# Fused gated linear attention and gated convolution network: the first k/q load behind a clearing, its multiplication in two, a fifth weight tile split without TensorE, and new instruction sequences

## The chip, the cores and the metric

The kernel runs on one core of one Trainium2 chip. The metric is the device time of one execution in microseconds (us); of several runs the median is taken. The core has five engines with instruction queues of their own: TensorE (PE in the profile, its weight loads PEld), VectorE (DVE), ScalarE (ACT), GpSimd (POOL) and SyncE (SP). An instruction starts when the ones before it on its engine have been issued and the semaphores that it waits for have come. DMA transfers are issued here by SP, and two of them by ScalarE; they run beside the engines.

## The reference

Inputs are q, k, v and f_logit of shape 4 x 8 x 768 x 48 (batch, heads, sequence, head size), and the weights moe_w_in (384 x 1024), moe_conv_w (3 x 1024) and moe_w_out (1024 x 384). The weights arrive as float64. Cut to what is computed:

```
f = 1 / (1 + exp(-f_logit))
for t in range(S):
    state = f[t] * state + outer(k[t], v[t])        # per batch and head, 48 x 48
    x[t]  = q[t] @ state                            # the heads side by side: 384 features
h    = relu(x @ w_in)                               # 768 x 1024 per batch
c[s] = conv_w[0]*h[s-1] + conv_w[1]*h[s] + conv_w[2]*h[s+1]
out  = (h * sigmoid(c)) @ w_out                     # 768 x 384 per batch
```

## The kernel before, in words

**Attention.** The sequence of each of the 4 batches is cut into 6 chunks of 128 positions: 24 steps n, each over all 8 heads (4 pairs p of heads). A step takes the logarithm of the gate (ScalarE, L532 Exp and L536 Ln), sums it along the chunk, forms e and its inverse (ScalarE, L567 with + and L569 with -, the two halves of tile e), and multiplies the k half and the q half of tile kq by them (VectorE, L573). For the steps of the first three groups (9 steps) the sum along the chunk is a TensorE product with a triangle of ones (L558, into a PSUM tile mm); for the others VectorE scans (L565). TensorE then turns k (L588, into PSUM tile Y; copied to kp by L599), forms the scores (L595, into S; masked into am by VectorE, L603), the rank products of k and v (L623), the products with the masked scores (L615) and with the carried state (L659). The state itself goes through L634, L636, L639 and L645. The result is kept as a high part (ScalarE, L672) and a low part (VectorE, L674) in xT, and six small DMAs (L682) gather the rest of the rows after every third step.

**Network.** For each half of a batch (384 positions) and each of 8 blocks of 128 inner features, nine products with high and low parts (L712) give h; ScalarE applies relu (L722) and the middle tap (L728), VectorE the two other taps (L732, twice), ScalarE the tanh of the gate (L736), VectorE the gate's product (L738). For each of 24 tiles of 128 positions ScalarE and VectorE form the high and low part (L755, L759), and 24 products (L768: 16 with the high part gh, 8 with the low part gl) give the output tile, which is copied (L774) and stored (L778). The first L768 of all needs all of w_out split.

**Splitting the weights.** A float64 weight is split into a high and a low part by integer operations (`split_f64`, L393 to L461). There are three tiles of w_in (two blocks of 512 columns each, 1024 elements a row) and four of w_out (768 elements a row). The character of `ez` for a tile sets its way. 'd': VectorE L418, L421, L431, L446; ScalarE L437 (high part); then for each of two halves TensorE joins three terms (L454 in fp32, L455 and L456 in fp32r) and ScalarE copies the sum out of PSUM (L459). 'r': VectorE L416, L418, L421, L424, L427, L429 and ScalarE L426; TensorE has no part in it. Before, the three tiles of w_in go by 'd' and the four of w_out by 'r'.

**What sets the order.** A planner (`class Plan`) holds every piece of work with its needs and buffers. `ORDER` (L35 on) lists them one after another; in `fixed` and `trace` they are issued in just this order, each into the queue of its engine, and a number behind a point says which buffer of a ring is taken. So `ORDER` fixes the sequence on every engine and of SP's DMAs. SP has at most 8 transfers under way: each DMA issue from the ninth on waits for the one eight before it.

**The start.** VectorE clears tile stir (L307), and TensorE multiplies it with itself (L383): two products of 512 and 320 columns and 12 more of 256 (`MORE`, L388), which compute nothing that is used; the planner places the 12 like other work. ScalarE's first instruction is the load of kq for step 0 (L379, 512 KB), its second the load of its function table (L380). SP begins with the gates of the first steps (L517, fb, 192 KB each).

## Time and profile before

| | |
|---|---|
| runs | 304.17, 305.18, 309.48 us; median 305.18 |
| profiled execution | 303.35 us, span 301.5 us (1.85 us lie around the span) |
| TensorE | busy 293.0 us, 97% of the span |
| VectorE | busy 254.1 us, 84% |
| ScalarE | busy 244.7 us, 81% |
| DMA | 43.38 MB, mean 144 GB/s over the span |
| granted TensorE clock | 1.00 (2.4 GHz) in all slices |

The profile shows one execution. Its page gives busy times, the span in slices, the chain of work that ended last, the costliest groups of instructions by line, and the DMA issues. Further views are asked of the same trace: the waits of an engine (who ended its idle time), the timeline (instructions in order of time), and the busy time of each engine in stretches. The sum of idle and busy time of the engine that is busy nearly always says what can be won from it; of another engine one reads when it has its results ready.

### The profile page before, as it was taken

The numbers are of one execution on the slowest core, as the hardware profiler recorded it, in microseconds if no ns is written. First come the engines' busy times: TensorE is split into PE (matmuls) and PEld (weight loads), VectorE is DVE, ScalarE is ACT, GpSimd is POOL, SyncE is SP. The second block draws the span as 40 slices with busy tenths as digits, with TensorE's granted clock in tenths as the row PEclk, the third lists the DMA queues.
The fourth block names the chain that finished last, engine by engine and source line by source line (L and its number), as shares of the span: only waits on it lengthen the run. The fifth ranks groups of instructions, "written<-read, shape, count | busy, mean of one in ns | idle before, by whom it ended". The sixth has DMA issues, their size and how long they took to land.

```text
span 301.5 us, 10045 instructions
## 1 busy us (share of the span) xinstructions
PE 293.0 (97%) x4319; PEld 275.4 (91%) x4319; DVE 254.1 (84%) x408; ACT 244.7 (81%) x493; POOL 2.8 (1%) x16
## 2 busy tenths in 40 slices
PE   6989999999999999999999999999999999999994
PEld 3877788999999999999999999999999999999993
DVE  3789999999999998998999997978796497599361
ACT  4778889999887999999899688796995877866740
POOL 3000000000000000000000000000000000000000
PEclk9999999999999999999999999999999999999999
DMA  7968699731420335742661236318340240323311
GB/s 257 390 248 260 206 309 400 216 110 44 120 86 1 99 109 163 222 157 72 231 174 68 72 73 208 107 47 267 113 143 11 73 150 0 116 103 123 96 54 58
DMA packets 19269, 43.38 MB, mean 144 GB/s; under 512 B 2685, under 2 KB 10005, under 8 KB 19221
## 3 DMA queue, kind: packets, MB, share of 16 engines
q1 hardware_dynamic: 18932, 41.98, 42.8%
q8 instruction: 35, 0.57, 0.8%
q10 hardware_dynamic: 288, 0.72, 0.7%
q14 instruction: 14, 0.11, 0.1%
HBM read 35.61 MB, written 4.72 MB: 134 GB/s over the span
## 4 chain that ended last, share of the span: by engine, by line
PE 88%; ACT 4%; DMA 3%; DVE 2%; SPq 1%; issue 1%; ACTq 0%
PE mm L712 33%; PE mm L768 32%; PE Y L615 4%; PE S L595 4%; PE Y L659 4%; PE Y L623 3%; PE Y L588 3%; PE mm L558 2%; DMA fb<-in_f_token_dram 1%; DMA v<-in_v_dram 1%; PE mm L454 1%; PE mm L383 1%; PE S L383 1%; ACT st L645 1%; DVE gl L759 1%
## 5 line engine op out<-in xcount | busy, mean ns | idle before, releaser
L712 PE MATMUL mm<-xT,wi 128*128 128x384 f32 x576 | 108.0, 341 | 0.0
L712 PEld LDWEIGHTS mm<-xT,wi 128*128 128x128 f32 x576 | 100.2, 188 | 1.5 <-ACT wi L459 0.4
L732 DVE SCALAR_TENSOR_TENSOR g<-hb,cw,g 128x384 f32<-128x384 f32 (+1 forms) x128 | 73.1, 615 | 6.0 <-ACT g L728 5.7
L768 PE MATMUL mm<-wo,gh 128*128 128x384 f32 x384 | 70.9, 338 | 0.0
L768 PEld LDWEIGHTS mm<-wo,gh 128*128 128x128 f32 x384 | 66.4, 188 | 0.3
L722 ACT ACTIVATE hb<-mm 128x384 f32<-128x384 f32 x64 | 31.1, 490 | 12.0 <-PE mm L712 11.4
L728 ACT ACTIVATE g<-hb,cw 128x384 f32<-128x384 f32 (+1 forms) x64 | 37.9, 614 | 1.4 <-DVE gl L759 1.2
L768 PE MATMUL mm<-wo,gl 128*128 128x384 f32 x192 | 37.2, 338 | 0.0
L759 DVE TENSOR_TENSOR gl<-g,gh 128x1024 fp32r<-128x1024 f32 (+2 forms) x28 | 29.4, 1065 | 8.6 <-PE mm L768 5.5
L738 DVE SCALAR_TENSOR_TENSOR g<-g,hb 128x768 f32<-128x768 f32 (+1 forms) x32 | 30.4, 956 | 4.3 <-ACT g L736 4.2
L768 PEld LDWEIGHTS mm<-wo,gl 128*128 128x128 f32 x192 | 33.4, 188 | 0.1
L736 ACT ACTIVATE g<-g 128x768 f32<-128x768 f32 (+1 forms) x32 | 27.0, 847 | 3.8 <-DVE g L732 3.7
L755 ACT CAST gh<-g 128x1024 fp32r<-128x1024 f32 (+2 forms) x28 | 25.8, 935 | 4.8 <-PE mm L768 3.6
L573 DVE TENSOR_TENSOR kq<-kq,e 128x1024 f32<-128x1024 f32 x24 | 29.0, 1217 | 0.0
L615 PE MATMUL Y<-am,v 64*64 64x64 f32 (+1 forms) x768 | 23.4, 219 | 0.0
L615 PEld LDWEIGHTS Y<-am,v 64*48 64x48 f32 (+1 forms) x768 | 18.8, 127 | 0.0
L603 DVE COPY_PREDICATED am<-mask,S 128x512 f32<-128x512 uint8 x24 | 17.6, 734 | 1.2 <-PE Y L615 0.7
L599 ACT COPY kp<-Y 128x512 f32<-128x512 f32 x22 | 12.8, 583 | 7.0 <-PE Y L588 7.0
L645 ACT ACTIVATE st<-st,ft_all 112x48 f32<-112x48 f32 x72 | 18.2, 329 | 0.0
L674 DVE TENSOR_TENSOR xT<-Y,xT 112x512 fp32r<-112x512 f32 x24 | 16.3, 684 | 2.2 <-ACT xT L672 2.1
L565 DVE TENSOR_TENSOR_SCAN fb<-runs,fb 128x512 f32<-128x512 f32 x15 | 18.0, 1213 | 0.0
L774 ACT COPY ob<-mm 128x384 f32<-128x384 f32 x21 | 10.0, 476 | 9.1 <-PE mm L768 7.2
(98 smaller groups left out, 355.2 us busy)
## 6 DMA issues: line engine op xcount, KB each, us to landing
kq<-in_kq_dram SPq DMA_DIRECT2D x22, 512.0 KB, 4.0
v<-in_v_dram SPq DMA_DIRECT2D x24, 192.0 KB, 4.8
out_dram<-ob SPq DMA_DIRECT2D x23, 192.0 KB, 2.5
kq<-in_moe_w_in_dram SPq DMA_DIRECT2D x6, 512.0 KB, 4.8
kq<-in_moe_w_out_dram SPq DMA_DIRECT2D x6, 512.0 KB, 3.7
xT<-xT SPq DMA_DIRECT2D x48, 48.0 KB, 3.2
fb<-in_f_logit_dram SPq DMA_DIRECT2D x9, 256.0 KB, 6.6
xT<-in_moe_w_in_dram SPq DMA_DIRECT2D x4, 512.0 KB, 6.0
```

The lines of the kernel that those rows point to most:

```text
L573: ox = plan.op("DVE", 1222, lambda e, X=X, E=E: nc.vector.tensor_tensor(buf(X), buf(X), buf(E), ALU.mult), ka, need=[o2] + ld_x, use=[X, E])
L615: o = nc.tensor.matmul(out_of(Y, p, j, w, z), buf(V).rearrange("p h d -> p (h d)")[t, h * D:h * D + w], buf(AM)[t, j, p, :], start=x == 1 ...
L645: o = nc.scalar.activation(new[:, p, :], new[:, p, :], AF.Copy, scale=ft_all[:HP + D, b, c, p:p + 1])
L712: nc.tensor.matmul(buf(ph)[:, :HS], wi[:, t, wl, f * P:(f + 1) * P], x_view(pl, u)[:, t, xl, :], start=(i == 0), stop=(i == 3 * KT - 1))
L722: nc.scalar.activation(hb[:, 2:HS + 2], buf(ph)[:, :HS], AF.Relu, scale=0.5)
L728: o = pl.op("ACT", 620, lambda e, cv=cv, hb=hb, n=n, f=f: nc.scalar.activation(cv(), hb[:, 1:n + 1], AF.Copy, scale=cw[:, 1, f:f + 1]), ke ...
L732: o = pl.op("DVE", 617, lambda e, cv=cv, hb=hb, n=n, f=f, w=w, sh=sh: nc.vector.scalar_tensor_tensor(cv(), hb[:, sh:n + sh], cw[:, w, f:f ...
L736: o = pl.op("ACT", 846, lambda e, cv=cv: nc.scalar.activation(cv(), cv(), AF.Tanh), key, need=last, use=[("g", u)], mode="T")
L738: gates[u, fp] = pl.op("DVE", 960, lambda e, cv=cv, fp=fp, n=n: nc.vector.scalar_tensor_tensor(cv(), cv(), 1.0, h_b[:, fp:fp + 2, 1:n + 1] ...
L755: o = pl.op("ACT", 180 + 110 * nn * NF // 128, lambda e, hv=hv, src=src: nc.scalar.copy(hv(), src()), key, need=[gates[v, fp] for fp in ra ...
L759: los.append(pl.op("DVE", 150 + 134 * nn * NF // 128, lambda e, hv=hv, lv=lv, src=src: nc.vector.tensor_tensor(lv(), src(), hv().bitcast(F ...
L768: nc.tensor.matmul(buf(po)[:, :DM], view(g)[:, f, :], wo[:, f, wl, :], start=(i == 0), stop=(i == 3 * NF - 1))
```

## The change

Four edits stand in the diff. First, the four kq buffers are made ahead; VectorE clears one column of the first between its clearings of the two am tiles, and ScalarE's load of kq for step 0 stands behind the load of its function table. As the load writes the buffer that VectorE cleared, it waits for that clearing. Second, for step 0 (`SPLIT = 1`) the multiplication of kq is two operations, k by the first half of e and q by the second; turning k needs only the first, the scores need both. Third, the third tile of w_in goes by 'r', so that five of seven tiles are split without TensorE. Fourth, `ORDER` is a new list. The diff, cut to its core (`ORDER` has 51 lines; the lines below it move by 4 to 6):

```diff
@@ CFG @@
+SPLIT = 1
...
-           m1d=19.03, m2=(14.064, -8.256, 111.289, 200.062, 301.175, 311.061, 558.989, 614.124), m2d=48.268, ez='dddrrrr')
+           m1d=19.03, m2=(14.064, -8.256, 111.289, 200.062, 301.175, 311.061, 558.989, 614.124), m2d=48.268, ez='ddrrrrr')
 
 ORDER = """
-139.0 91.0 92 100.1 93 45.0 157.1 23.1 94 140.0 95.0 10.0 24 96 102 141.0 97.1 103 101 8.1 142.0 0.0 98 159.1 143 46.0
...
+137.0 89.0 43.0 90 91 23.1 98.1 24 92 156.1 93.0 9.1 138.0 139.0 174.2 0.0 140.0 99 8.1 94 2.0 143 157.1 44.0 7.1 95.0
...
@@ -333,8 +334,10 @@
     plan, serial = Plan(tc), count()
     am_b = [sb([P, 2, NP, HP], f"am{i}") for i in range(2)]
-    for t in am_b:
-        nc.vector.memset(t, 0.0)
+    kq_b = [sb([P, 2, NP, P], f"kq{i}") for i in range(4)]
+    nc.vector.memset(am_b[0], 0.0)
+    nc.vector.memset(kq_b[0][:, 0, 0, :1], 0.0)
+    nc.vector.memset(am_b[1], 0.0)
...
-    for nm, n, shape in (("fb", 2, [P, GC, NP, P]), ("kq", 4, [P, 2, NP, P]), ("v", 4, [P, H, D]), ("e", 2, [P, 2, NP, P]),
+    for nm, n, shape in (("fb", 2, [P, GC, NP, P]), ("v", 4, [P, H, D]), ("e", 2, [P, 2, NP, P]),
                          ("kp", 2, [P, NP, P])):
...
+    plan.ring("kq", [(t, [("kq", i)]) for i, t in enumerate(kq_b)])
...
     moe_rings(plan, wk, ps)
-    kq0 = nc.scalar.dma_start(plan.rings["kq"][0][0], kq_in[0, 0])
     nc.scalar.preload_act_table_set("natural_log_exp_and_others")
+    kq0 = nc.scalar.dma_start(kq_b[0], kq_in[0, 0])
...
-        ox = plan.op("DVE", 1222, lambda e, X=X, E=E: nc.vector.tensor_tensor(buf(X), buf(X), buf(E), ALU.mult), ka,
-                     need=[o2] + ld_x, use=[X, E])
+        oq = [plan.op("DVE", 690 if n < SPLIT else 1222, lambda e, X=X, E=E, z=z: nc.vector.tensor_tensor(
+            buf(X)[:, z], buf(X)[:, z], buf(E)[:, z], ALU.mult), ka, need=[d] + ld_x, use=[X, E])
+            for z, d in (((0, o1), (1, o2)) if n < SPLIT else ((slice(0, 2), o2),))]
+        ox = oq[-1]
...
-        o = plan.op("PE", 436, turn, (n, "tu"), need=[ox], use=[X], take=[("Y", Y)], mode="t", n=8)
+        o = plan.op("PE", 436, turn, (n, "tu"), need=[oq[0]], use=[X], take=[("Y", Y)], mode="t", n=8)
...
-        o = plan.op("PE", 490, score, (n, "sc"), need=[ox], use=[X], take=[("S", SC)], mode="q", n=64)
+        o = plan.op("PE", 490, score, (n, "sc"), need=oq, use=[X], take=[("S", SC)], mode="q", n=64)
```

Some places in the sequences, as they come out of the build. ScalarE's start, with what each instruction waits for (fb are the gates, fg their logarithms, mm the sums along the chunk, kq and e as above; DMAHW, DVE, PE, Pool and Activation name the semaphore's source). Before:

```order
L379 DMA kq_112<-in_kq_dram 128x1024
L380 ACT_TABLE_LOAD
L532 ACTIVATE fb_110<-fb_110 128x384 [waits DMAHW1_49]
L536 ACTIVATE fg_124<-fb_110 128x8x48 [waits Activation_49,Pool_49]
L532 ACTIVATE fb_110<-fb_110 128x384 [waits DMAHW2_49]
L536 ACTIVATE fg_125<-fb_110 128x8x48 [waits Activation_49,Pool_49]
L532 ACTIVATE fb_111<-fb_111 128x384 [waits DMAHW3_49]
L567 ACTIVATE e_120<-mm_128 128x512 [waits PE_49]
```

and with the change:

```order
L383 ACT_TABLE_LOAD
L384 DMA kq_90<-in_kq_dram 128x1024 [waits DVE_49]
L536 ACTIVATE fb_115<-fb_115 128x384 [waits DMAHW0_49]
L540 ACTIVATE fg_125<-fb_115 128x8x48 [waits Activation_49,Pool_49]
L571 ACTIVATE e_121<-mm_129 128x512 [waits PE_49]
L536 ACTIVATE fb_115<-fb_115 128x384 [waits DMAHW3_49]
L417 ACTIVATE gh_168<-xT_142 24x128 [waits DMAHW1_49]
L540 ACTIVATE fg_125<-fb_115 128x8x48 [waits Activation_49]
L573 ACTIVATE e_121<-mm_129 128x512 [waits PE_49]
```

The load of kq stands behind the table load and has a wait on VectorE; the first half of e for step 0 (L571) stands ahead of the second gate.

TensorE at the same place, from the second sum along the chunk on (L383 and L387 are the products of stir, L588 and L594 the turning of k, L595 and L601 the scores). Before:

```order
L558 MATMUL mm_129<-tri_73,fg_125 128x128 x4
L383 MATMUL S<-stir 128x256 x2
L558 MATMUL mm_128<-tri_73,fg_124 128x128 x4
L383 MATMUL S<-stir 128x256
L588 MATMUL Y_108<-ident,kq_112 128x128 x4
L595 MATMUL S<-kq_112 64x64 x16
```

and with the change:

```order
L562 MATMUL mm_129<-tri_73,fg_125 128x128 x4
L387 MATMUL S<-stir 128x256
L594 MATMUL Y_113<-ident,kq_90 128x128 x4
L387 MATMUL mm_130<-stir 128x256
L601 MATMUL S<-kq_90 64x64 x16
L562 MATMUL mm_129<-tri_73,fg_125 128x128 x4
```

The third sum has moved behind the scores of step 0. Of the 12 products of stir, 6 stand ahead of the first turning before and 7 with the change; the last one stood at 62.4 us before, among the attention steps, and stands now far behind the last step, between products of the network.

VectorE ahead of the first output product: the last pieces of the split of w_out (L429 and L433 write wo). Before:

```order
L427 TENSOR_SCALAR gh_1363<-gh_1363 128x768
L427 TENSOR_SCALAR gh_878<-gh_878 128x768
L429 SCALAR_TENSOR_TENSOR wo<-gl_1391,gh_1363 128x2x384
L603 COPY_PREDICATED am_88<-mask_85,S 128x512
L699 MEMSET hb 128x2x2
L429 SCALAR_TENSOR_TENSOR wo<-gl_874,gh_878 128x2x384
L565 SCALAR_TENSOR_TENSOR fb_110<-runs,fb_110 128x512
```

and with the change:

```order
L433 SCALAR_TENSOR_TENSOR wo<-gl_1036,gh_1064 128x2x384
L428 SCALAR_TENSOR_TENSOR gl_1345<-gl_1345,xT_832 128x768
L431 TENSOR_SCALAR gh_1372<-gh_1372 128x768
L705 MEMSET hb 128x2x2
L433 SCALAR_TENSOR_TENSOR wo<-gl_1345,gh_1372 128x2x384
L569 SCALAR_TENSOR_TENSOR fb_115<-runs,fb_115 128x512
```

One mask of a score (L603) has moved behind the last piece. Between the first product of kq and the last piece of wo VectorE has otherwise the same operations but for two small ones, and those that 'r' adds for the tile that now goes by it. In SP's queue both loads of the first tile of w_in (512 KB each) now stand ahead of the kq load for step 1, where one stood behind it and one behind the first v, and the first five of the six gathers of the first half (L682) follow one another without another load between them.

## Rows read from the trace of the kernel before

**Rows 1.** The page, busy time of each engine (us, share of the span, instructions):
```profile
PE 293.0 (97%) x4319; PEld 275.4 (91%) x4319; DVE 254.1 (84%) x408; ACT 244.7 (81%) x493; POOL 2.8 (1%) x16
```
**Rows 2.** Waits of TensorE: who was waited for, us in total, times, longest:
```profile
PE mm L558 <- ACT fg L536: 1.3, 1, 1.3
PE Y L623 <- issue: 1.0, 1, 1.0
```
**Rows 3.** Timeline of the start: start and length in us, engine, line, operation, [idle before]:
```profile
0.88 0.40 ACTq L379 DMA_DIRECT2D kq<-in_kq_dram  x1
0.91 1.83 SPq L517 DMA_DIRECT2D fb<-in_f_token_dram  x4
1.20 3.99 PE L383 MATMUL mm<-stir 128*128 128x512 f32 x6 [1.20 <-DVE stir L307]
1.20 1.02 DVE L337 MEMSET am<- 128x512 f32 x2
1.31 1.28 ACT L380 ACT_TABLE_LOAD   x1 [1.31 <-PEq L975]
...
5.14 0.33 SPq L549 DMA_DIRECT2D v<-in_v_dram  x1
5.34 0.52 ACT L532 ACTIVATE fb<-fb 128x384 f32<-128x384 f32 x1 [2.75 <-DMA fb<-in_f_token_dram]
...
6.53 1.16 PE L558 MATMUL mm<-tri,fg 128*128 128x128 f32 x8 [1.34 <-ACT fg L536]
...
7.83 0.58 ACT L567 ACTIVATE e<-mm 128x512 f32<-128x512 f32 x1
...
10.24 1.21 DVE L573 TENSOR_TENSOR kq<-kq,e 128x1024 f32<-128x1024 f32 x1
...
11.50 0.66 PE L588 MATMUL Y<-ident,kq 128*128 128x128 f32 x4
```
**Rows 4.** Waits of SP's DMA queue up to 40 us:
```profile
SPq L549 <- DMA kq<-in_kq_dram: 1.0, 1, 1.0
```
**Rows 5.** Stretches of the start: busy us by engine, clock, DMA share, GB/s:
```profile
1.50:3.00 1.50, 1.50 (x2) 0.53 (x2) 1.45 (x8) 1.09 (x1) 1.47 (x8) 1.00 0.57 109
1.50:4.50 3.00, 3.00 (x5) 1.54 (x5) 2.26 (x10) 1.09 (x1) 1.86 (x10) 1.00 0.77 246
```
**Rows 6.** DMA issues: engine, KB each, median us from issue to landing:
```profile
out_dram<-ob ACTq DMA_DIRECT2D x1, 192.0 KB, 1.9
```
**Rows 7.** Timeline of TensorE: one join between its neighbours; the critical chain's product of stir:
```profile
30.08 1.02 PE L454 MATMUL mm<-gh,ident 128*128 128x512 f32 x2
...
31.50 0.62 PE L623 MATMUL Y<-v,kp 64*64 64x48 f32 x30
...
62.59 0.43 PE S L383 x2
```
**Rows 8.** Groups by line and shape on VectorE: count, busy us, mean ns, idle before:
```profile
L603 DVE COPY_PREDICATED am<-mask,S 128x512 f32<-128x512 uint8 x24 | 17.6, 734 | 1.2 <-PE Y L615 0.7 <-PE S L595 0.3
L674 DVE TENSOR_TENSOR xT<-Y,xT 112x512 fp32r<-112x512 f32 x24 | 16.3, 684 | 2.2 <-ACT xT L672 2.1
L421 DVE SCALAR_TENSOR_TENSOR gh<-xT,gh 128x1024 int32<-128x1024 int32 x2 | 2.5, 1225 | 0.0
L418 DVE TENSOR_SCALAR gh<-xT 128x1024 int32<-128x1024 int32 x2 | 1.3, 672 | 0.0
```
**Rows 9.** Timeline around the first output product:
```profile
93.05 0.95 DVE L429 SCALAR_TENSOR_TENSOR wo<-gl,gh 128x768 fp32r<-128x768 f32 x1
...
94.35 2.94 PE L768 MATMUL mm<-wo,gh 128*128 128x384 f32 x16
```
**Rows 10.** From the first product of kq to the last wo, columns as rows 5:
```profile
11.45:94.00 82.55, 81.05 (x1476) 71.70 (x1476) 79.57 (x132) 72.10 (x156) 0.00 (x0) 1.00 0.60 200
```
**Rows 11.** Waits of VectorE in that stretch, the two longest:
```profile
DVE sh L636 <- PE Y L615: 1.0, 2, 0.8
DVE am L603 <- PE Y L615: 0.7, 1, 0.7
```

More of the change, by code (lines that the diff above doesn't have):

```diff
@@ L85 @@
-649 650 1213 653 1204 1219 1214.0 646 654 1206.1 1220v.1 1222.1 647 1221 1215 655 1203.1 1224.0 659 1223.0 1205 651
-1207 1225 1208.1 1209 1226v.0 1227
[23 rows of a table added]
+836 407.0 845 837 379 865v 363 442 867 395.0 408 365 364 424 871.0 422.2 409 443.1 444 793v.0 380 794 878 410 879.1
[4 rows of a table added]
+858 861.0 460 441.1 890 876 434 420.0 877 477.1 478 913 136 435 862 943 895 896 944.1 421 863v.0 462 902 949.0 531
+447.1 450.1 945 437 448.0 956 903 907 465.0 474.2 436v 438 451 914 950 975.1 439 461 969 466.0 452 908 463.0 918.0 453
@@ new lines @@
+464.0 467 492.1 909 864 957.0 468 493 946.0 469 475.1 479v 495 976 915 962.1 480 958 977 496.0 916 970.0 454 612 549
[5 rows of a table added]
+1014 601 967 942 530.0 993 602 968 603 534 1010.1 523 934 604 994 1059.0 1026.0 935v.1 524 551 1020v 1015 553 536.1
+526 537.0 1011 1027 556.0 651.3 525 1012 540 936 1016 527.1 600 1021.0 1046 1017 1028 599 541 1018 557.0 1029 1034.1
+1022 528 1023 618 554.0 542 623.2 1024 1052.0 555.0 1019 652 1041 543v 558 1053 1035 544 559 1036 1025 560 631.0 1054
[8 rows of a table added]
+1076 1185 1199 1167 1143.0 1155.0 1077v.0 1171 1078 655.1 1154 1172 1139.1 1156 1144.0 1186 1157 1158 1159 1140 1200
@@ L87 @@
+1160 1187 1145.0 1141.0 1173 1142 1161 1174 1209.1 1146 1215.0 1210.1 1211.1 1147.0 1216.0 641 1148 648 1212 1201.1
+1217.0 1213.0 1202.1 1203 656 1218 1221.0 657 1223.1 1222.0 1219.1 649 1220 1214 658 552v 650 1204 642 1205.0 646 1206
+1224 1207.0 1208 11.0 1225v.0 1226
 """
```

6 lines of the change are left out of this document (removed), and 81 rows, old and new, of the table ORDER.

## The prediction

> **What bounds the kernel now.** I read the page's busy times first. TensorE is busy 293.0 us of a span of 301.5 us, 97% [rows 1], at the granted clock 1.00 throughout, so the first question is what its idle time and its work are made of. Its waits [rows 2] are few. It waits 1.34 us for the first gate before the first sum along the chunk, and 0.98 us once with nothing to wait for ("issue"). The other idle time lies before 1.20 us and behind its last product. The chain of waits says the same, so a gain must be work that TensorE is spared or one of those two waits, and a loss must be a new wait.
>
> The second question is who keeps up with TensorE. From the end of the first product of kq (11.45 us) to the last piece of wo (94.00 us) VectorE is busy 79.57 of 82.55 us and TensorE 81.05 [rows 10]. Both are full. The last piece of wo ends at 94.00 and the first output product, which needs it, starts at 94.35 [rows 9]: VectorE is just in time there. So whatever makes TensorE earlier than VectorE by that place is lost there.
>
> **The fifth tile without TensorE.** It removes two joins from TensorE, each a product in fp32 and two in fp32r. One join takes from 30.08 to 31.50, 1.42 us, to the start of the next work [rows 7], so two are 2.84 us, all of them on the bound engine. ScalarE loses two copies out of PSUM, which I count at nothing, as it is not the last to arrive in the stretches I looked at; if that cover went, it would be a gain. VectorE gets one more operation of the kind of L418 (0.672) and one more of the kind of L421 (1.225), together 1.90 us [rows 8]; the other four operations of the tile correspond in kind and size. These 1.90 us lie in the full stretch of VectorE.
>
> **The first load behind a clearing.** Before, ScalarE issues the 512 KB of kq at 0.88 and SP the first gate (192 KB) at 0.91. SP's wait for that kq load ends at 5.14 [rows 3, 4], and the gate's Exp starts at 5.34, so the two land together, though one is 2.7 times the other. By 3.0 us 0.16 MB had moved and by 4.5 us 0.74 MB (109 GB/s over 1.5 us, 246 over 3.0 [rows 5]), which is about the 0.72 MB of the two; from there to the landing it takes another 0.7 us. With the change the table load is first (0.88 to 2.16 with the 1.28 us of [rows 3]), the clearing is over at about 1.8 (two clearings of am take 1.02 from 1.20, the column comes after the first), and the kq load is issued between 1.8 and 2.2. Its first bytes follow about 1.1 us later, as those of the first loads do. By then the 0.197 MB of the gate have had the engines to themselves: at the 0.16 MB that had moved by 3.0 they are through at about 3.2, and land at 3.95.
>
> Bounds of that landing: 2.8 (0.91 and the 1.9 us of the 192 KB that ScalarE stores at the end [rows 6]) and 5.34 (nothing changes). I take 3.95, which goes by the bytes of this very start. The Trainium skill (DMA: Bandwidth & Descriptors, section "Queues, rings and completion order") says that each DMA engine takes turns between queues packet by packet, and that a transfer's semaphore comes only after all earlier writes of that engine, whatever their queue. By that rule the small gate lands with the big kq load that was issued first, as the trace shows, and the landing moves with the change; were the queues independent of each other, it would stay at 5.34 and the sum would be that of the first rival.
>
> From the landing to the first sum it takes 1.19 us (5.34 to 6.53 [rows 3]): 5.14 instead of 6.53. TensorE's opening products of stir last to 5.19 [rows 3], so its wait of 1.34 us is gone. An earlier landing than 4.0 brings TensorE no more.
>
> **The multiplication in two.** The first half of e starts 1.30 us after the sum (6.53 to 7.83): 6.5. The k half can be multiplied from 7.1 to 7.8 (0.684 for 512 columns, from the nearest operation of this size, L674 [rows 8]). The kq load, 4.26 us on its way before (0.88 to 5.14), lands at 6.1 to 6.5, in time. On ScalarE four more instructions, about 0.4 us apart (one of them 0.2), bring the second half of e to 8.6; the q half ends at 9.3. Before, the whole product ended at 11.45. The two halves cost VectorE 0.16 us more than the one of 1.21 and the column 0.07.
>
> TensorE, in its new order, does not turn k at 7.8: five products of stir (0.43 each [rows 7]) and the second sum (0.9) are ahead of the turning, which makes 5.19 + 0.9 + 5 x 0.43 + 0.9 + 0.43 = 9.6. In one operation the product would have ended at 9.9; the division itself is worth 0.3 us to TensorE at most.
>
> **The new sequences.** All 12 small products of stir remain; one moves from 62.4 us to far behind the first output product, which is 0.43 us less before that place and the same total. On VectorE one mask (0.73 [rows 8]) moves behind the last piece of wo. SP's queue has both loads of a w_in tile ahead of the kq load of step 1. Up to the first v it then issues 2.6 MB, with kq of step 0 3.1 MB. At the 383 GB/s that rows 5 give between 3.0 and 4.5 us, v lands at about 11.4; it is wanted at about 12.2, behind turning, scores and third sum, so I count it at nothing. The six gathers start when VectorE has the third xT, about as late as before, but are issued without the two loads between them; I count them at nothing as well. For the rest the work per engine is the same in kind and number, and behind the last attention step TensorE's sequence is that of before.
>
> **The sum.** At the first output product TensorE would be 1.34 + 2.84 + 0.43 = 4.61 us earlier, at 89.74. VectorE's last piece of wo would be ready at 9.3 + 79.57 + 1.90 - 0.73 = 90.04 if it never waits, and at 93.0 if it waits 2.98 us, as before. Of these, 1.7 us were waits for TensorE [rows 11], which is now further ahead of VectorE than it was; I take them as gone and keep 1.28: 91.3. So TensorE waits 1.6 us (bounds 0.3 and 3.3). To the end: 4.61 - 1.6 - 0.43 = 2.6 us. From the profiled execution's 303.35 us that is **300.8 us**, between 299.5 (VectorE never waits) and 302.4 (it waits as before). The runs shown have their median 1.8 us above the profiled execution and their lowest 0.8 above; for a median I add 0.7 and say 301.5.
>
> **The rivals.**
> *The gate lands no earlier.* Then 1.34 us stay with TensorE, and VectorE starts 1.4 us later: 91.1 for TensorE, 92.7 for VectorE, again 1.6 us of waiting, and 302.1 is left. For it: the DMA engines stood half idle up to 3.0 us [rows 5], so the gate's landing may be a matter of starting up and not of sharing. Against it: two loads of such different size landing together. In this case the wait does not do what its place suggests. Chance 0.15.
>
> *The kq load comes late, and the kernel is slower.* The load now starts when SP has begun to fill the DMA engines. VectorE's queue has the whole rest behind its k half: the q half, the convolution weights, the first w_in tile, every later product. If it landed last of all that SP has under way (3.1 MB), it would land at 11.4; the q half would end near 13.3, the last piece of wo at 95.3, TensorE would wait 5.6 us there, and the time would be 304.8. It is slower than before from a landing at 10.0 on. Against it: before, the load got through in 4.26 us beside SP's loads. Chance 0.1.
>
> *VectorE is no gate and TensorE's wait for "issue" goes too.* The 0.98 us stood at 18.47 us, and which instruction it meets depends on the sequence. Without both, 303.35 - 1.34 - 2.84 - 0.98 = 298.2; with one of them between that and 299.5. For it: VectorE's waits are mostly waits for TensorE. Against it: nothing in the change removes the wait for "issue". Chance 0.15.
>
> The forecast (299.5 to 302.4) has 0.55, and 0.05 is left for a collision that I have not seen, such as a late v or gather somewhere in the new order, of either size.
>
> **How the numbers follow.** The range reaches from 298.4, close to the third rival, to 305.2, a little over the second rival. Two per cent, about what a measurement of this kernel can tell from no change, is 6.1 us: faster would be below 299.1, slower above 311.3. Faster takes most of the third rival, 0.12; slower only a part of what I have not seen, 0.03; the rest, 0.85, is within.
>
> **What would show it.** In the trace after: the first gate's Exp near 4.0 us (5.3: first rival); no wait of TensorE before the first sum; the k half at about 7.1, the q half done by 9.3 (near 12 or later: second rival); the first turning near 9.6; four joins, not six; the last piece of wo near 91 and the first output product right behind it, with a wait of TensorE of 0.3 to 3.3 us before it or in the steps that lead there. If TensorE instead waits in many places for VectorE or for loads, and the sum of these waits is over 4 us, the forecast is wrong.

## The result: 0.6% slower, where 1% faster was forecast

| | before | changed |
|---|---|---|
| median of 13 runs each, us | 305.27 | 307.35 |
| changed to before | | 1.0062, 95% interval 1.0034 to 1.0091 |
| profiled execution, us (span) | 303.35 (301.5) | 304.30 (302.6) |
| TensorE idle in the span, us | 8.5 | 12.3 |

The loss is within the 2% that one calls no change, but it is one, and the time lies above the range forecast (298.4 to 305.2). (Comparisons leave disturbed runs out.) The lines of the file moved: L558 is now L562, L573 L577, L588 L594, L595 L601, L615 L621, L623 L629, L659 L665, L712 L718, L768 L774, L429 L433.

The page of the changed kernel, its busy times (answers to [rows 1]) and the first line of the chain that ended last:

```profile
PE 290.3 (96%) x4311; PEld 274.7 (91%) x4311; DVE 256.5 (85%) x416; ACT 241.0 (80%) x485; POOL 2.8 (1%) x16
...
PE 89%; DVE 4%; DMA 2%; issue 2%; SPq 1%; ACT 0%; DVEq 0%
```

TensorE's work fell by 2.7 us, as the two joins should give. Its idle time rose by 3.8. The waits of TensorE (answers to [rows 2]):

```profile
PE Y L629 <- issue: 2.0, 2, 1.4
PE S L601 <- issue: 1.8, 1, 1.8
PE mm L562 <- issue: 1.3, 1, 1.3
PE mm L387 <- DVE stir L308: 1.2, 1, 1.2
PE Y L665 <- DVE st L645: 0.9, 2, 0.5
PE mm L562 <- ACT e L573: 0.7, 1, 0.7
PE S L601 <- DVE kq L577: 0.6, 1, 0.6
```

The wait for the first gate (1.34) is gone. In its place stand 5.1 us of waits for "issue", for which the profile names nothing, against 0.98 before, and 2.2 us of waits for VectorE and ScalarE. The start itself went about as forecast (timeline of ScalarE, then of VectorE; answers to [rows 3]):

```profile
0.88 1.28 ACT L383 ACT_TABLE_LOAD   x1 [0.88 <-PEq L981]
1.73 0.40 ACTq L384 DMA_DIRECT2D kq<-in_kq_dram  x1
3.34 0.52 ACT L536 ACTIVATE fb<-fb 128x384 f32<-128x384 f32 x1 [1.18 <-DMA fb<-in_f_token_dram]
...
8.02 0.57 ACT L573 ACTIVATE e<-mm 128x512 f32<-128x512 f32 x1
```
```profile
6.88 0.69 DVE L577 TENSOR_TENSOR kq<-kq,e 128x512 f32<-128x512 f32 x1 [3.06 <-DMA kq<-in_kq_dram]
...
8.68 0.67 DVE L577 TENSOR_TENSOR kq<-kq,e 128x512 f32<-128x512 f32 x1
```

The gate's Exp starts at 3.34 (before 5.34), the k half at 6.88 with its load as the last to come, and the q half ends at 9.35. By the first output product everything is lost (VectorE, then TensorE; answers to [rows 9]):

```profile
94.97 0.96 DVE L433 SCALAR_TENSOR_TENSOR wo<-gl,gh 128x768 fp32r<-128x768 f32 x1
```
```profile
96.19 1.54 PE L774 MATMUL mm<-wo,gh 128*128 128x384 f32 x8
```

Before, that product started at 94.35. TensorE does not wait there: it comes 1.8 us later by itself. Here are the four waits for issue, in the timeline of TensorE:

```profile
18.44 0.40 PE L629 MATMUL Y<-v,kp 64*64 64x48 f32 x15 [0.68 <-issue]
...
24.49 0.61 PE L629 MATMUL Y<-v,kp 64*48 64x48 f32 x29 [1.36 <-issue]
...
40.29 0.60 PE L562 MATMUL mm<-tri,fg 128*128 128x128 f32 x4 [1.30 <-issue]
...
46.68 0.33 PE L601 MATMUL S<-kq 48*64 48x64 f32 x3 [1.76 <-issue]
```

Each stands in the middle of a run of equal small products, where nothing new is needed. What they share is their place in the count. The stretches from 0 to each of them (busy us and, in brackets, the instructions recorded):

```profile
0.00:18.43 18.43, 15.29 (x221) 11.90 (x222) 13.28 (x33) 13.52 (x31) 2.76 (x16) 1.00 0.89 324
0.00:24.48 24.48, 19.52 (x349) 15.63 (x349) 18.50 (x41) 17.46 (x43) 2.76 (x16) 1.00 0.89 322
0.00:40.28 40.28, 33.56 (x731) 27.39 (x732) 33.12 (x64) 30.62 (x74) 2.76 (x16) 1.00 0.79 273
0.00:46.67 46.67, 38.19 (x857) 31.62 (x858) 37.16 (x69) 35.92 (x85) 2.76 (x16) 1.00 0.82 289
```

Products and weight loads of TensorE together: 443, 698, 1463, 1715. The differences are 255, 3 times 255, and 252. These views leave out the semaphore and control instructions in TensorE's queue; with them the trace has 449, 705, 1473 and 1729 instructions ahead of the waits, exactly 256, 3 times 256, and 256 apart. The wait of before stands behind 444, or 449 with them. So TensorE seems to wait every time at the end of a block of 256 instructions. The page has a DMA queue that would bring them: `q8 instruction`, 35 packets, 0.57 MB, 16 KB each; 8,622 instructions of TensorE make 33.7 blocks of 256.

**Theory F**: TensorE's instructions come in blocks of 256 through the DMA engines; where TensorE runs through a block faster than the next one comes, it waits, and what made it faster is given back. **Rival S**: the waits belong to the new sequence, that is to the instructions that wait and to something that their new places make late.

### The profile page after: what moved, and what is told of

The parts are those of the page before. It is cut to its first block, busy times and chain, and to the rows that moved or that the text cites. A ratio compares the mean times of both kernels' runs of the same rounds, so it can differ in the third digit from the quotient of the medians.

```text
span 302.6 us, 10048 instructions
## 1 busy us (share of the span) xinstructions
PE 290.3 (96%) x4311; PEld 274.7 (91%) x4311; DVE 256.5 (85%) x416; ACT 241.0 (80%) x485; POOL 2.8 (1%) x16
## 4 chain that ended last, share of the span: by engine, by line
PE 89%; DVE 4%; DMA 2%; issue 2%; SPq 1%; ACT 0%; DVEq 0%
PE mm L774 33%; PE mm L718 32%; PE Y L665 4%; PE Y L629 4%; PE Y L621 4%; PE S L601 4%; PE Y L594 3%; DMA xT<-in_moe_w_in_dram 2%; PE mm L562 2%; DVE g L738 1%; PE mm L458 1%; DVE g L744 1%; SPq L521 1%; PE mm L387 0%; DVE xT L680 0%
## 5 line engine op out<-in xcount | busy, mean ns | idle before, releaser
L718 PE MATMUL mm<-xT,wi 128*128 128x384 f32 x576 | 108.1, 340 | 0.1
L718 PEld LDWEIGHTS mm<-xT,wi 128*128 128x128 f32 x576 | 100.2, 188 | 1.4 <-ACT hb L728 0.4
L738 DVE SCALAR_TENSOR_TENSOR g<-hb,cw,g 128x385 f32<-128x385 f32 (+1 forms) x128 | 73.1, 614 | 4.4 <-ACT g L734 3.8
L774 PE MATMUL mm<-wo,gh 128*128 128x384 f32 x384 | 71.1, 338 | 0.0
L774 PEld LDWEIGHTS mm<-wo,gh 128*128 128x128 f32 x384 | 66.3, 188 | 0.4
L774 PE MATMUL mm<-wo,gl 128*128 128x384 f32 x192 | 37.3, 338 | 0.0
L774 PEld LDWEIGHTS mm<-wo,gl 128*128 128x128 f32 x192 | 33.4, 188 | 0.1
L577 DVE TENSOR_TENSOR kq<-kq,e 128x1024 f32<-128x1024 f32 (+1 forms) x25 | 29.2, 1172 | 3.2 <-DMA kq<-in_kq_dram 3.1
L621 PE MATMUL Y<-am,v 64*64 64x64 f32 (+1 forms) x768 | 23.4, 219 | 0.0
L605 ACT COPY kp<-Y 128x512 f32<-128x512 f32 x24 | 14.0, 584 | 9.0 <-PE Y L594 8.5
L601 PE MATMUL S<-kq 48*64 48x64 f32 x768 | 17.2, 221 | 2.3 <-issue 1.8
L621 PEld LDWEIGHTS Y<-am,v 64*64 64x64 f32 (+1 forms) x768 | 18.7, 127 | 0.0
L629 PE MATMUL Y<-v,kp 64*64 64x48 f32 (+1 forms) x704 | 16.4, 214 | 2.1 <-issue 2.0
```

The costliest lines, as they stand in the source:

```text
L577: oq = [plan.op("DVE", 690 if n < SPLIT else 1222, lambda e, X=X, E=E, z=z: nc.vector.tensor_tensor(buf(X)[:, z], buf(X)[:, z], buf(E)[:, ...
L601: o = nc.tensor.matmul(scores()[t, j, p, :], buf(X)[r, 0, p, t], buf(X)[r, 1, p, t], start=True, stop=True)
L621: o = nc.tensor.matmul(out_of(Y, p, j, w, z), buf(V).rearrange("p h d -> p (h d)")[t, h * D:h * D + w], buf(AM)[t, j, p, :], start=x == 1 ...
L629: nc.tensor.matmul(pk(z)[HP * j:HP * j + w, p, :], buf(KP)[t, p, HP * j:HP * j + w], buf(V)[t, 2 * p + j, :], start=True, stop=True)
L718: nc.tensor.matmul(buf(ph)[:, :HS], wi[:, t, wl, f * P:(f + 1) * P], x_view(pl, u)[:, t, xl, :], start=(i == 0), stop=(i == 3 * KT - 1))
L738: o = pl.op("DVE", 617, lambda e, cv=cv, hb=hb, n=n, f=f, w=w, sh=sh: nc.vector.scalar_tensor_tensor(cv(), hb[:, sh:n + sh], cw[:, w, f:f ...
```

## The experiments

Ratios are to the kernel before, run on the same chip in the same session; chip or session differ between the changed kernel, e1 to e4, e5 to e8, e9 to e12, e13 to e15, and e16 with e17. "Issue" is the sum of TensorE's waits for issue up to 60 us in the profiled execution, which is one execution; in e7 and e13 it is the slowest of the runs (318.42 and 309.32 us).

| run | edit | ratio, 95% interval | median | issue |
|---|---|---|---|---|
| changed | | 1.0062, 1.0034 to 1.0091 | 307.35 | 5.1 |
| e1 | changed, 64 more instructions at the start | 1.0373, 1.0338 to 1.0408 | 316.3 | 6.2 |
| e2 | before, tile edit alone | 1.0092, 1.0057 to 1.0126 | 307.42 | 1.2 |
| e3 | before, first edit alone | 1.0014, 0.9985 to 1.0042 | 305.21 | 1.3 |
| e4 | changed without the first edit | 1.0089, 1.0056 to 1.0122 | 307.87 | 5.4 |
| e5 | changed, loads under way limited to 1030 KB | 1.0361, 1.0322 to 1.0399 | 316.77 | 1.4 |
| e6 | the same, 1540 KB | 1.0024, 0.9994 to 1.0055 | 306.41 | 2.1 |
| e7 | before, 1030 KB | 1.0327, 1.0277 to 1.0377 | 315.84 | 0 |
| e8 | changed, two stirs twice as long | 1.0101, 1.0066 to 1.0135 | 308.32 | 4.9 |
| e9 | changed, two loads of w_out later | 0.9999, 0.9963 to 1.0035 | 305.09 | 3.2 |
| e10 | e9 and two more loads later | 1.0064, 1.0035 to 1.0093 | 306.52 | 3.6 |
| e11 | e10 and two of w_in later | 1.0047, 1.0019 to 1.0075 | 306.13 | 3.7 |
| e12 | changed, multiplication in one | 1.0107, 1.0071 to 1.0143 | 307.52 | 4.8 |
| e13 | changed, one slow product ahead of the scores | 1.0035, 1.0007 to 1.0063 | 305.97 | 5.6 |
| **e14** | e9 and e13 together | **0.9938, 0.9916 to 0.9961** | 302.90 | 1.7 |
| e15 | e14 and one stir earlier | 0.9941, 0.9918 to 0.9964 | 303.44 | 1.7 |
| e16 | e14 without the first edit | 0.9949, 0.9911 to 0.9987 | 304.14 | 1.8 |
| e17 | e14, multiplication in one | 0.9930, 0.9890 to 0.9969 | 303.30 | 1.7 |

### Are the waits tied to the count? (e1)

```diff
-    for i, n in enumerate(STIR):
-        stirred(plan.rings["mm"][i][0], n)
+    stirred(plan.rings["mm"][0][0], STIR[0])
+    for i in range(17):
+        nc.tensor.matmul(plan.rings["mm"][1][0][:48, :64], stir[:48, :48], stir[:48, :64], ...)
```

> The changed kernel, except that the second opening product of stir (320 columns) is replaced by 17 small ones (48x48 by 48x64), which puts 64 more instructions on TensorE ahead of everything else in about the same time. Theory F (TensorE's instructions arrive in blocks of 256 and the waits for 'issue' are waits for the next block): the waits for issue of over 0.5 us stand again behind about 443, 698, 1463 and 1715 recorded instructions, or other members of 443 + 256 k, that is at work 64 instructions earlier in the program than before the edit, and their sizes differ. Rival S (the waits belong to the new sequence: the instruction that waits is held by something that its place in the sequence makes late): the same instructions wait as in the changed kernel, now behind about 507, 762, 1527 and 1779 records, with the same sizes within 0.3 us. Time: F 0 to 3 us below the changed kernel, or up to 1 above; S the same within 0.5.

The timeline of TensorE in e1, and the stretches up to its first four waits for issue:

```profile
20.70 0.33 PE L622 MATMUL Y<-am,v 64*64 64x64 f32 x6 [0.76 <-issue]
...
26.75 0.70 PE L622 MATMUL Y<-am,v 64*48 64x64 f32 x16 [1.81 <-issue]
...
44.93 0.20 PE L630 MATMUL Y<-v,kp 64*48 64x48 f32 x1 [0.89 <-issue]
...
54.21 0.34 PE L622 MATMUL Y<-am,v 64*64 64x64 f32 x2 [2.72 <-issue]
```
```profile
0.00:20.69 20.69, 18.72 (x222) 15.11 (x222) 11.23 (x30) 11.29 (x24) 2.77 (x16) 1.00 0.76 274
0.00:26.74 26.74, 22.39 (x349) 18.28 (x350) 16.88 (x40) 14.57 (x33) 2.77 (x16) 0.98 0.80 284
0.00:44.92 44.92, 39.22 (x731) 32.31 (x732) 30.51 (x59) 28.70 (x71) 2.77 (x16) 0.92 0.67 233
0.00:54.20 54.20, 45.77 (x857) 38.26 (x858) 36.26 (x67) 36.26 (x85) 2.77 (x16) 0.93 0.72 250
```

444, 699, 1463, 1715 (with all instructions 449, 705, 1473 and 1729, as in the changed kernel): the same counts, now at other instructions, 64 earlier in the work. S falls: behind the 64 instructions the sequence is the same, and the waits did not go with it. The expectation on the time was wrong: the small products took 3.86 us where the large one took about 1, and the products of stir behind them ran slowly for longer (last section). The time says nothing of F.

### When does a block come?

Times of the `q8` packets, found by narrowing windows of the DMA view to 0.06 us, beside the ends of TensorE's waits:

| | packet starts, us | TensorE goes on, us | between |
|---|---|---|---|
| before | 16.97 | 19.45 | 2.48 |
| changed | 16.02, 22.03, 37.85, 44.26 | 18.44, 24.49, 40.29, 46.68 | 2.42, 2.46, 2.44, 2.42 |
| e1 | 18.19, 24.31, 42.25, 51.72 | 20.70, 26.75, 44.93, 54.21 | 2.51, 2.44, 2.68, 2.49 |

TensorE goes on 2.4 to 2.7 us behind the start of a packet, each time. So the wait is for that packet. Before, the next two packets start at 21.19 and 26.12 and TensorE is through with its block at 23.46 and 28.71, 2.3 and 2.6 us later: it just did not wait. That the old sequence stood at this edge no view that I read for the prediction showed.

And when does a packet start? In the changed kernel TensorE crosses a block's end at 18.44; the packet for the block after the next end starts at 22.03, 3.6 us later. At 70.35, with no data on the way, it takes 0.6 us. The queues, from 18.45 to 22.05 and 22.05 to 23.25, then from 70.92 to 72.0:

```profile
q1 hardware_dynamic: 361, 1.08, 87.0%
```
```profile
q1 hardware_dynamic: 104, 0.33, 79.5%
q8 instruction: 1, 0.02, 5.5%
```
```profile
q8 instruction: 1, 0.02, 8.0%
```

In the first of them 1.08 MB of data move and no instruction packet. The other lags between 12 and 50 us in this kernel are 1.9 to 4.0 us, but for one packet that starts 0.6 us ahead of its block's end, where the block ends in slow products; so it seems to be asked for some instructions ahead of the end. How busy the DMA engines are does not settle the lag alone: at 59.42 us it is 0.7 us beside gathers of xT and a load of v (DMA share 1.01, 203 GB/s), at 35.16 us 2.7 us beside loads (0.77, 243 GB/s).

### The parts alone (e2, e3, e4, e12)

e2 and e3 are the kernel before with one edit each (`ez='ddrrrrr'`, the tile's six operations in the places of those they replace; the first edit's lines of the diff). e4 takes the first edit back in the changed kernel, e12 sets `SPLIT = 0` there.

> The kernel before, with the fifth weight tile split without TensorE and nothing else changed (its sequence kept, the tile's own operations in the places of those that they replace). Two joins (2.84 us) leave TensorE. F: TensorE is further ahead and reaches the ends of its instruction blocks earlier, so the waits for issue rise from 1.0 us to 2 or more and 0.5 to 2 us of the 2.84 are gained. S (the loss comes from the new sequences): the waits for issue stay at 1.0 us and 2.3 to 2.8 us are gained.

> The kernel before, with the first edit alone (table load, then the kq load behind the clearing); sequence and tiles kept. The gate's Exp starts near 3.4 instead of 5.34 and the 1.34 us wait for the first gate goes. F: the end of the first watched block (record 443) is reached that much earlier and the wait for issue there grows from 1.0 to about 2; the gain is 0 to 0.6 us. S: the wait stays at 1.0 and the gain is 1.0 to 1.3 us.

> The changed kernel with the first edit taken back (the kq load ahead of the table load, no clearing of its column); new sequence, halves and tile kept. The gate's Exp is back near 5.3. F: TensorE starts 0.8 to 1.4 us later, and gets this back in smaller waits for issue at the first two block ends; time within 0.5 us of the changed kernel. S: 0.8 to 1.4 us slower than the changed kernel.

> The changed kernel with the first multiplication of k and q in one operation again (it stands where the q half stood; sequence otherwise kept). The k turning at 10.07 us then waits for the whole product, which ends near 10 us. Prediction's step: the division is worth 0.3 us to TensorE at most there; F: that is given back or taken by the first wait for issue, and the time is the changed kernel's within 0.5 us. S: up to 0.5 us slower.

Neither theory had e2 right: it is 0.9% slower with 1.2 us of waits for issue, near the 1.0 of S and not the 2 or more of F. The longest wait of TensorE in e2:

```profile
PE Y L588 <- DVE xT L674: 2.8, 1, 2.8
```

VectorE has 1.9 us more to do ahead of the low part xT, which frees the PSUM tile that the turning needs: 41.09 instead of 37.93. Another 1.1 us come from a wait for issue after all: TensorE waits 1.01 us at 30.39, and VectorE's mask behind it 1.82 us instead of 0.73. In the old places the tile's work on VectorE is on the path; in the changed kernel, with the new list, this wait does not appear. e3 gains nothing, though its gate is at 3.40. One wait went and another came, on ScalarE and then on TensorE:

```profile
7.81 0.52 ACT L535 ACTIVATE fb<-fb 128x384 f32<-128x384 f32 x1 [2.25 <-DMA fb<-in_f_token_dram]
8.24 0.58 ACT L570 ACTIVATE e<-mm 128x512 f32<-128x512 f32 x1
```
```profile
PE mm L561 <- ACT fg L539: 1.2, 1, 1.2
```

The third gate's load came late, and the first e of step 0 was queued behind its Exp. e4 has its gate at 5.20 again, TensorE waits 1.39 us for it, and the ratio is 0.3% above that of the changed kernel, with overlapping intervals; the time doesn't tell the theories apart. e12 is at 1.0107, 0.45% above the changed kernel, more than either theory had, and its interval overlaps too; with most waits for issue gone nothing of this is left (e17). One expectation of F failed in both: a later TensorE was to wait less at the first block ends, and it waits more at the first two (0.91 and 1.91 us in e4, 0.93 and 1.90 in e12, against 0.68 and 1.36), though the wait near 40 us is gone. What TensorE loses ahead of a block's end does not simply come back at it; when the packet starts counts as well.

### Work in the gap (e8)

```diff
-(stirred(plan.buf(("z", i))[:, 0] if ring == "S" else plan.buf(("z", i)), 256),) * 2,
+(stirred(plan.buf(("z", i))[:, 0] if ring == "S" else plan.buf(("z", i)), 512 if i in (3, 6) else 256),) * 2,
```

> The changed kernel, except that two of its small products of stir (those at 21.40 and 36.95 us, in the stretches that end in the waits for issue at 24.49 and 40.29) have 512 columns instead of 256: 0.43 us more of TensorE work each, no instruction more. F: both waits shrink by about 0.43 us each, to 0.9, and end at the same times; span unchanged within 0.3 us. S: the waits keep their sizes and what follows each comes 0.43 us later; span +0.86.

The two waits shrank to 1.20 and 1.02, by 0.16 and 0.28 instead of 0.43 each, and the span rose by 0.7, near the 0.86 of S. The waits did not end at the same times either (24.90 and 40.97): the packets came later as well (22.28 and 38.51). The first wait, ahead of both edits, rose by 0.21 (0.89 against 0.68), so one trace against another is not fine enough to weigh such differences. This run doesn't support F; most of the work that was put into the gaps was paid for.

### Less on the way (e5, e6, e7)

SP issues a load only when the sizes of those under way leave room for it:

```diff
+            if "SP" in o.engs and o.size and len(sent) < 40:
+                room, k = 1030 - o.size, len(sent)          # e6: 1540
+                while k and room >= sent[k - 1].size:
+                    k -= 1
+                    room -= sent[k].size
+                o.after = sent[k - 1] if k else None
+                sent.append(o)
```

> The changed kernel, except that SP issues each of its first 40 loads only when no more than 1030 KB would be on their way (before, some 2 MB are). TensorE's, VectorE's and ScalarE's sequences are the same. F with contention (an instruction block's transfer starts 0.5 to 0.9 us after TensorE crosses a block's end where the DMA engines are quiet, and 2 to 4 us after it between 12 and 50 us, where loads fill them): the transfers start within about 2 us, and the waits for issue fall from 5.1 us to 0 to 2.5; the time falls by 1 to 4 us unless loads come late, which the trace would show as waits for DMA. S, or blocks that come at a pace of their own whatever the loads do: waits for issue still about 5 us, time the same or later by late loads.

> As the run with 1030 KB, with 1540 KB allowed on the way. F with contention: between the changed kernel and the other limit, waits for issue of 1.5 to 4 us, and fewer late loads. S: 5 us of issue and the time of the changed kernel.

> The kernel before, with the same limit of 1030 KB on SP's first 40 loads. F with contention: its one wait for issue (0.98 us) goes or halves, gain up to 1 us if no load is late. Otherwise: 0.98 us stay, and a loss where loads come late.

The waits for issue fell to 1.4, 2.1 and 0, but loads came late (waits of TensorE in e5, then in e6):

```profile
PE Y L636 <- DMA v<-in_v_dram: 9.9, 4, 4.4
```
```profile
PE Y L636 <- DMA v<-in_v_dram: 3.8, 3, 1.7
PE Y L636 <- issue: 1.7, 2, 1.1
```

A TensorE that waits for v also gives the next block more time, so these runs don't separate the two. They show that the limit of 1030 KB costs far more than it brings (3.6% and 3.3% above the kernel before). With 1540 KB the ratio is 0.4% below the changed kernel's, but the intervals overlap.

### Loads moved singly (e9, e10, e11)

Only places in `ORDER` change: e9 has `53.2 54` (w_out) behind `211.0` (a v load), e10 also `63 62` behind `263.2`, e11 also `34.0 35` (w_in) behind `100`.

> The changed kernel, except that SP issues its first two loads of w_out (384 KB each, issued at 16.33 and 18.01 us and first used at 31.27) six loads later, near 25 us, when the DMA engines stand half empty. No engine's sequence changes but SP's. F with contention: the block that lands at 24.49 is on its way while these 768 KB are; its transfer starts earlier than 22.06, the wait of 1.36 us shrinks by 0.5 to 1.3, those before it stay; time 0.3 to 1.3 us below the changed kernel. S: the wait stays 1.36, the time as in the changed kernel.

> As before it, and the next two loads of w_out (issued at 37.8 and 38.9 us, first used at 49.41) behind the kq and v loads at 45 us. F with contention: the wait of 1.30 us at 40.29 stays (its block's transfer starts at 37.84, as these loads begin), the one of 1.76 at 46.68 shrinks by 0.5 to 1.7, since its transfer (44.25) waits behind fewer bytes; time another 0.3 to 1.5 us lower, unless w_out is then late for VectorE at 49.4. S: waits and time as in the changed kernel.

> As before it, and the two loads of the third w_in tile (issued at 9.11 and 9.9 us, 1 MB, first used at 20.54) behind the v load and the gate at 12.2 us. F with contention: the block that lands at 18.44 is asked for near 13 us with fewer bytes ahead of it, the wait of 0.68 us there goes or halves, that at 24.49 may grow back; v of step 0 and 1 come earlier. S: all waits for issue stay.

In e9 the second packet starts at 21.04, 2.4 us behind the block's end (18.66) instead of 3.6, and the wait of 1.36 is gone; so is that of 1.30 behind it, while the first and the last grew (0.68 to 0.96 and 1.76 to 2.27). That is F with contention for the packet that was aimed at: 768 KB moved, no sequence but SP's touched, and the ratio 0.6% below that of the changed kernel. Up to 60 us two waits for issue are left:

```profile
18.66 0.40 PE L629 MATMUL Y<-v,kp 64*64 64x48 f32 x15 [0.96 <-issue]
...
45.49 0.33 PE L601 MATMUL S<-kq 48*64 48x64 f32 x3 [2.27 <-issue]
```

For e10 and e11 the expectation failed. The waits at 46 us (1.76 and 1.36) and at 19 us (1.07 and 1.05) stayed, the one near 40 us was back (0.78 and 1.31), and a new one came (TensorE for ScalarE's copy of wi, 1.96 and 1.01 at 55.6 and 55.9). So the bytes on the way are not all that delays a packet; what else does is open.

After the wait of 2.27 us the granted clock of e9 falls. The stretch behind that wait, in e9 and in e14:

```profile
45.49:52.00 6.51, 6.50 (x67) 4.74 (x66) 5.72 (x8) 3.02 (x5) 0.00 (x0) 0.74 0.95 361
```
```profile
45.32:52.00 6.68, 6.33 (x80) 4.47 (x80) 6.19 (x10) 4.64 (x7) 0.00 (x0) 1.00 0.90 336
```

A mean of 0.74 over 6.5 us is a mixture of the upper level (2.4 GHz) and the lower (1.2 GHz), ahead of which TensorE stood idle. It costs e9 about 1.7 us of TensorE's busy time (292.9 against 291.2 in e14). The same fall stands in e4 (behind a wait of 2.54 us), e12 (2.00), e16 (1.57) and e11 (1.36), not in the profiled executions of the changed kernel (1.76) and of e10 (1.76); so the length of this wait alone does not decide it. Single runs scatter with it: the four runs of e9 with a mean clock of 0.998 or more took 302.4 to 303.0 us, the other eight 304.9 to 306.5. Of the changed kernel's 13 runs eleven had a mean clock of 0.982 to 0.994; of the 29 runs of the kernel before beside e9, 27 had 0.997 or more (19 of 21, 19 of 23, 26 of 29 and 19 of 23 in the other sessions). That the clock falls behind 46.68 in those runs I take from e4 and e9; no trace of such a run of the changed kernel was there.

### A slow product in the block (e13, e14, e15)

In e13 `691.1` (nine matmuls of L718, 1.6 us in 18 instructions) stands ahead of `253.0` (the scores in whose middle the fourth wait lies) instead of four places behind it. e14 has this and e9's loads. e15 has e14 and `3.0` (a stir) ahead of the first block end.

> The changed kernel, except that one product for the convolution (nine matmuls of L718, about 1.6 us, 18 instructions; it starts at 46.94, right behind the wait of 1.76 us) stands ahead of the scores in whose middle that wait falls. F: the slow product fills the time in which the next block is on its way; the wait shrinks by 1.2 to 1.7 us and nothing is paid for it; the other waits for issue stay; time 1 to 3 us below the changed kernel (the higher figure if the granted clock then no longer falls behind 47 us). S: the scores are late by 1.6 us, the wait moves with them, and the time is the changed kernel's or more.

> Both: the first two loads of w_out near 25 us and the product ahead of the scores. F: of the four waits for issue only the first (0.7 to 1.0 us) is left at size, the granted clock stays at its upper level throughout, and the time is 1 to 4 us below the kernel before (301 to 304 median). S: no more than the run with the loads alone gave (the time of the kernel before).

> As before it, and one small product of stir (0.43 us, 21.40 us in the changed kernel) ahead of the block end at 18.4 us instead of behind it. F: the first wait for issue shrinks by 0.3 to 0.5 us and the product is no longer paid for behind it; 0.2 to 0.5 us less. S: no difference, or 0.4 us more.

e13's fourth wait fell from 1.76 to 0.97, less than the 1.2 to 1.7 expected; its second, expected to stay, rose to 3.55 in the one trace that I have, with its packet at 24.95. That trace is of e13's slowest run, and says little of the others. The ratio is between the changed kernel's and e9's. e14, with the same operations as the changed kernel, is 0.6% faster than before. The page's busy times of e14, its larger waits for issue, and VectorE and TensorE at the first output product:

```profile
PE 291.2 (97%) x4311; PEld 274.4 (91%) x4311; DVE 256.3 (85%) x416; ACT 240.8 (80%) x485; POOL 2.8 (1%) x16
```
```profile
18.54 0.40 PE L629 MATMUL Y<-v,kp 64*64 64x48 f32 x15 [0.85 <-issue]
...
45.32 0.39 PE L601 MATMUL S<-kq 48*64 48x64 f32 x11 [0.67 <-issue]
```
```profile
93.14 0.96 DVE L433 SCALAR_TENSOR_TENSOR wo<-gl,gh 128x768 fp32r<-128x768 f32 x1
```
```profile
94.23 2.94 PE L774 MATMUL mm<-wo,gh 128*128 128x384 f32 x16
```

Its last piece of wo ends at 94.10 and the product starts at 94.23. With the waits for issue mostly gone VectorE is just in time there, as before. So the lead at this place is 0.12 us (94.23 against 94.35), and not the 4.61 us that the prediction gave TensorE. The two profiled executions differ by 0.66 us (302.69 and 303.35), most of it behind this place, and the medians by 2.0 us; what the slower runs of the kernel before do, most of them at a mean clock of 0.997 or more, no trace shows. Against e9 the difference goes with the clock: the four runs of e9 at 0.998 or more (302.4 to 303.0 us) are as short as e14's twelve (302.1 to 304.2), all of which are at 0.997 or more. e15 brings no more: the first wait fell to 0.36 as expected, and the second came back with 0.74.

### What the parts are worth then (e16, e17)

> The kernel with both moves (two w_out loads later, the product ahead of the scores), with the first edit taken back: the kq load ahead of the table load, no clearing of its column. The gate's Exp is then back near 5.3 us and TensorE waits about 1.3 us for it. F: some 0.7 to 0.9 of these come back at the first block end (whose wait of 0.85 us shrinks), and 0.4 to 0.7 us is lost against the kernel with both moves. S: all of it is lost, 1.2 to 1.4 us.

> The kernel with both moves, with the first multiplication of k and q in one operation. The prediction gave the division 0.3 us at most. F: what is lost ahead of the first block end comes back there: 0 to 0.3 us slower than with the division. S: 0.3 to 0.5 us slower.

e16: the gate's Exp is at 5.43 and TensorE waits 1.43 us for it, and its first wait for issue is 0.20 instead of 0.85. So 0.65 of it came back at the block's end, as F has it, but the wait of 0.67 at 45.32 is 1.57 here (at 47.66), and the clock falls behind it. Both ratios are within the interval of e14: what the first edit and the division are worth in the time is below what these runs can tell, about 0.4%.

## Why the prediction was wrong, step by step

- **The gate.** Right, and earlier than forecast (3.34 against 3.95; with the first edit taken back, 5.20 in e4); the wait of 1.34 us went. The k half (6.88 against 7.1), the q half (9.35 against 9.3) and the first turning (10.07 against 9.6) are near. The second sum waited 0.71 us for ScalarE's second e, as its PSUM tile was not free; that I had not seen.
- **The joins.** Right in size: TensorE is busy 2.7 us less (2.84 forecast).
- **The step that failed** is the sum: "At the first output product TensorE would be 1.34 + 2.84 + 0.43 = 4.61 us earlier". I let each microsecond that TensorE is spared become a lead that only VectorE, at the last piece of wo, could take back. TensorE came there at 96.19, 1.8 us later than before: its work up to that place is 2.8 us less (87.5 against 90.3), its idle time 4.6 us more (8.7 against 4.0). Its instruction blocks took the lead on the way: the waits for issue rose from 0.98 to 5.1 us, at the ends of blocks that it now reaches sooner or at a worse time for the fetch. e1 and the packets show what is waited for. Why each of these packets is too late is only in part known. The two joins that are gone were slow work with few instructions (1.42 us each, at 33.63 and 38.16 before), but only the wait of 1.30 ends a block that lost one. The block that ends in the wait of 1.76 has nine of the products L718 (1.8 us, from 41.09), where the block that ended at 46.53 before had 18 (3.4 us, from 41.65): that the new list did. The block that ends in the wait of 1.36 has no less work than before (4.2 us, before 4.1); its packet started 3.6 us behind the block's end ahead of it, where the one of before took 1.7.
- **"For the rest the work per engine is the same in kind and number"**, so the new sequences counted at nothing. On TensorE it is also a question of how many instructions stand between two slow products, as the nine products of L718 show. The 2.2 us of new waits for VectorE and ScalarE were left out as well; they stay in e14 (0.9, 0.7 and 0.6).
- **VectorE's gate** is the second term that failed, though it did not set the time here. From the end of the q half (9.35) to the last piece of wo (95.93 instead of 91.3) VectorE works 80.67 us, as forecast (79.57 + 1.90 - 0.73 = 80.74), but it waits 5.9 us instead of 1.28. The two longest names of these waits are the loads of w_in (up to 10.48 and 42.48), for which VectorE did not wait before between 11.45 and 94.00, and which the prediction did not count, and the scores behind the block's end at 46.68:

```profile
DVE gh L422 <- DMA xT<-in_moe_w_in_dram: 1.6, 2, 1.0
DVE am L609 <- PE S L601: 1.5, 1, 1.5
```

  The last piece is 0.26 us ahead of TensorE, before it was 0.35. In e14, with most waits for issue gone, VectorE waits 4.6 us, its last piece comes at 94.10, and in the last 34.1 us up to there it is busy for all but 0.06. So, as far as e14 shows, VectorE would have taken most of the lead even if TensorE had kept it, and the bound "it waits as before" (93.0) was too early too.
- **The rivals.** The third had the wait for issue in its hands, but only as something that might go; "nothing in the change removes the wait for 'issue'" was true, and the question that belonged beside it, what would add to it, was not asked. The sentence on waits of TensorE that sum to over 4 us describes what came, but names VectorE and loads as their cause.
- **The median** stands 3 us above the profiled execution (forecast: 0.7 above). The lower clocks of most runs, behind such waits, fit that. So the traces show about 1 us of the loss (303.35 to 304.30), and the clock is the likely rest of the 2.1 us between the medians; that is argued, not shown.
- Behind the first output product the changed kernel takes 0.7 us less than before (206.4 against 207.1). The sum took 0.43 us off the gain for the product of stir that moved. But that product does not stand between products of the network: it starts at 298.24 us, behind the last matmuls of the last output product (297.68), where nothing waits for it. Another 0.2 us is a wait for a v load (at 155.63 before) that is gone. The rest I have not taken apart.

## What to carry to other kernels

Where a bound engine has waits that the profile puts down to nothing, count its instructions up to them. If the counts lie 256 apart, look up the instruction packets in the DMA view and how close the other blocks come to them, before work is taken off that engine: slow instructions between runs of small ones seem to have bought the time for the next block here. Then try to move loads that aren't needed yet out of the stretches in which blocks are fetched, and slow products into them; here moving two loads and one product turned the changed kernel from 0.6% slower to 0.6% faster by the median. It has to be tried: two further moves of loads did not help (e10, e11), and two longer products in the gaps were mostly paid for (e8). No run has the moves in the kernel before, so how much of the 0.6% needs the four edits is not shown; without the first edit or the division it is the same within 0.4% (e16, e17).

## What the runs showed of the hardware that was not expected

- Instructions of TensorE cost waiting time at block ends, 5.1 us here. The Trainium skill (Runtime: NRT & Kernel Launch, section "Instruction fetch mechanics") says that the engine fetches them in 16 KiB blocks of 256 while it executes the current one, and that crossing a boundary is mostly hidden. The trace agrees on the blocks (449, 705, 1473 and 1729 instructions, 16 KB packets). It differs on the cost: 5.1 us of waits in the changed kernel, single ones of 0.7 to 2.7 us there and in e1. The measurement decides.
- In the changed kernel a block's packet starts 0.6 us behind a block end where nothing else moves (70.35), and mostly 1.9 to 4.0 us behind it among loads; where TensorE waited for it, it goes on 2.4 to 2.7 us after the packet's start.
- In e1 the products of stir stay slow for longer. The timeline of TensorE: the first of these are 0.86 us apart, the last 0.44, though the profile gives a granted clock of 1.00 for both. In the changed kernel they are 0.43 apart from 5.61 on. Why is open.

```profile
9.71 1.06 PE L387 MATMUL S<-stir 128*128 128x256 f32 x2
10.57 1.06 PE L387 MATMUL mm<-stir 128*128 128x256 f32 x2
...
12.27 0.60 PE L387 MATMUL mm<-stir 128*128 128x256 f32 x2
12.71 0.59 PE L387 MATMUL S<-stir 128*128 128x256 f32 x2
```
